# Later weight loads, an earlier load of the last w2 blocks, q units moved ahead and statistics reordered, in a one-core attention and MLP kernel

## The chip, the cores and the metric

The kernel runs on one core of one Trainium2 chip. The metric is device time in microseconds (us) of one execution. Each execution also has a span (first to last instruction, about 1.8 us shorter than the device time) and a mean granted TensorE clock. The highest clock recorded is 1.00, called full clock here; the lowest in any stretch read is 0.50, called half clock.

Engine names in the profile: PE is TensorE (matrix products), PEld its weight loads, DVE is VectorE, ACT is ScalarE, POOL is GpSimd, SP is the engine that issues most DMAs here (SPq in the timeline). L558 means line 558 of the kernel. Names such as `RB`, `OTR` or `yT` are buffers of the kernel; `OTR` receives the transposed attention output. PE writes its products to `ps_all`, a buffer in PSUM that the kernel divides into banks of 512 columns.

## The reference

One sequence of 2048 tokens, width 576, 32 heads of 18, MLP width 4608, bfloat16:

```python
def _A_ref(x, wqkv, w_phi, wo):              # linear attention with learned features
    q, k, v = ...                            # x @ wqkv, split into heads
    pq = einsum("bhsd,hdf->bhsf", q, w_phi)  # the same for k: pk
    phi_q = concatenate([softmax(pq), softmax(-pq)])   # the same for k: phi_k
    kv = einsum("bhsf,bhsd->bhfd", phi_k, v)
    z  = einsum("bhsf->bhf", phi_k)
    o = einsum("bhqf,bhfd->bhqd", phi_q, kv) / (einsum("bhqf,bhf->bhq", phi_q, z) + 1e-6)
    return merge_heads(o) @ wo
def _B_ref(x, w1, b1, w2, b2):               # MLP, with its own layernorm
    return gelu(layernorm(x) @ w1 + b1) @ w2 + b2
h  = x + _A_ref(layernorm(x), A_wqkv, A_w_phi, A_wo)
h2 = h + _B_ref(layernorm(h), B_w1, B_b1, B_w2, B_b2)
```

## The kernel before

The tokens are 16 tiles of 128. There are four stages.

1. Preparation (to 12 us): x and weights arrive, the k weights are multiplied by w_phi ("weffk").
2. The kv loop (12 to 81 us): per tile a layernorm, a transpose of the normed tile (`yT`), the k product (L558), its exponentials on ACT (L565), the v product (L574), and the accumulation of kv (L609). Between them stand the weffq units (L487, L493), and then "q units" (L639): products whose exponentials (L645, on ACT) give Eq for attention.
3. A short chain to W1 (81 to 103 us): attention and output product of tiles 0 and 1, and the remaining q units.
4. Eight rounds of W1 and W2, some 39 us each, with the attention of later tiles woven in.

A helper records every operation, works out its waits from what it reads and writes, and leaves each engine's program in the order of the calls. So order is all that the change edits. In the loop, `t` is the tile and NT is 16. The parts that it touches (cut):

```python
    def ln1_stats_act(t):     # mean and square sum on ACT (L362, L364), four small POOL operations
    def ln1_stats_dve(t):     # the same by bn_stats on DVE, two small POOL operations
    def ln1_norm(eng, t):     # ybuf = (x - mean) * rstd (L390)
    def ln1_tr(t):            # yT(t) = transpose of ybuf by DMA, issued on SP
    def ln1_petr(t, col):     # the same on PE (L425) with a copy on ACT (L429)
    def fill(n, banks):       # the next n q units, their PSUM banks in turn
    ...
    WU = {2: (0, 1), 3: (2, 3), 4: (4, 5, 6)}
    for t in range(NT):
        for u in ((4, 5) if t == 1 else (t + 4,) if 1 < t < NT - 4 else ()):
            ln1_norm("pool", u)
        p1_k(t)               # L558, L565
        if t == 0:
            p1_v(0)
            ln1_petr(1, 512 * 6)
        if t == 1:
            ln1_petr(2, 512 * 6)
        ... weffq units, fill(1) from tile 5, p1_v(t - 1), p1_kv(t - 2) ...
        for u in ((4, 5) if t == 1 else (t + 4,) if 1 < t < NT - 4 else ()):
            ln1_tr(u)
        if t == 1:
            ln1_stats_act(6)
        elif t % 2 == 1 and t + 5 < NT:
            ln1_stats_act(t + 5)
        ... p1_mul(t - 1), p1_sums(t) on DVE ...
        if t == 0:
            ln1_stats_act(4)
            ln1_stats_dve(5)
        elif t % 2 == 0 and t + 5 < NT:
            ln1_stats_dve(t + 5)
        if t == 1:
            ... two DMA transposes of b1, on SP ...
        if t >= 1 and bulk:   # 18 loads: w1, wo, first w2 blocks, b2; on SP
            bulk.pop(0)()
        if t >= 1 and t % 4 == 0 and bulk:
            bulk.pop(0)()
    p1_v(NT - 1, 0); p1_kv(NT - 2); p1_mul(NT - 1, 0)
    fill(2, (4, 3))
    p1_kv(NT - 1)
    ...
    fill(3, QB2)
    attn_oT(0, S1)            # transpose on PE, copy on ACT
    y0 = attn_wo(0, S1, True) # output product L754, then DVE
    attn_oT(1, S2)
    fill(1, QB2)
    y1 = attn_wo(1, S2, True)
    fill(24, QB2)             # all that are left
    attn_yT(y0, ...); attn_yT(y1, ...)
    attn_N(2, S1)             # attention product L659 of tile 2, then DVE, POOL, DMA transpose
    ... load the last 16 w2 blocks (2 x 1152 KB) on SP ...
```

The softmax here doesn't subtract the row's maximum and nothing guards it: scores larger than these inputs give would overflow.

Of the kernel before, what the change touches and what calls it, by code (L numbers as in the profile page):

```python
# [185 lines left out]
def _build(nc, A_x, A_wqkv, A_w_phi, A_wo, B_w1, B_b1, B_w2, B_b2, out):  # L186
# [6 lines left out]
    NT = S // 128  # L193
# [17 lines left out]
    def hap(t, row, off, dims, np_=128):  # L211
        return bass.AP(t, off, [[row, np_]] + [list(d) for d in dims])
# [18 lines left out]
    NW2B = 16  # L231
# [3 lines left out]
    wv = RB[:, 0:2880].rearrange("p (c f) -> p c f", c=5)  # L235
    Ek = [RB[:, 2880 + ES * i:2880 + ES * (i + 1)] for i in range(3)]
    VO = 2880 + 3 * ES
    vext = [RB[:, VO + 1216 * i:VO + 1216 * (i + 1)] for i in range(2)]
    wkst = w2a[:, 0:6, :].rearrange("p m d -> p (m d)")[:, 0:3200].rearrange("p (c k) -> p c k", c=5)
    w2b = RB[:, 0:NW2B * D].rearrange("p (m d) -> p m d", m=NW2B)  # L240
# [36 lines left out]
    def res(name):  # L277
        if name not in R:
            R[name] = Res(name)
        return R[name]  # L280
# [38 lines left out]
    def load(q, dst, src, writes, reads=()):  # L319
        ch = P.chan(f"ld{nch[0]}", q)  # L320
        nch[0] += 1
        P.dma(ch, lambda e: e.dma_start(dst, src), reads=reads, writes=writes)
# [36 lines left out]
    def ln1_stats_act(t):  # L359
        s, w = res(f"s1a{t}"), res(f"s1b{t}")  # L360
        st = lambda k: st1[:, k, t:t + 1]
        P.add("act", lambda e: e.activation(junk[:, 0, :], x_all[:, t, :], AF.Copy, scale=1.0 / D, accum_out=st(6)),  # L362
              reads=[res(f"x{t}")], writes=[s, res("junk0")])
        P.add("act", lambda e: e.activation(junk[:, 1, :], x_all[:, t, :], AF.Square, scale=float(D) ** -0.5,  # L364
                                            accum_out=st(1)),
              reads=[res(f"x{t}")], writes=[s, res("junk1")])
        P.add("pool", lambda e: e.tensor_tensor(st(2), st(6), st(6), ALU.mult), reads=[s], writes=[w])
        P.add("pool", lambda e: e.tensor_tensor(st(7), st(1), st(2), ALU.subtract), reads=[s, w], writes=[w])
        P.add("pool", lambda e: e.tensor_scalar(st(4), st(7), EPS, None, ALU.add), reads=[w], writes=[w])
        P.add("pool", lambda e: e.tensor_tensor(st(5), st(4), neghalf[:, 0:1], ALU.pow),  # L370
              reads=[w, res("neghalf")], writes=[w])

    def ln1_stats_dve(t):
        s, w = res(f"s1a{t}"), res(f"s1b{t}")
        for i in range(2):
            P.add("dve", lambda e, i=i: e.bn_stats(bns[:, 6 * i:6 * i + 6], x_all[:, t, 288 * i:288 * i + 288]),
                  reads=[res(f"x{t}")], writes=[res("bns")])
        P.add("dve", lambda e: e.bn_aggr(hap(st1, 8 * NT, 6 * NT + t, [[NT, 2]]), bns[:, :]),
              reads=[res("bns")], writes=[s])
        P.add("pool", lambda e: e.tensor_scalar(st1[:, 4, t:t + 1], st1[:, 7, t:t + 1], EPS, None, ALU.add),  # L380
              reads=[s], writes=[w])
        P.add("pool", lambda e: e.tensor_tensor(st1[:, 5, t:t + 1], st1[:, 4, t:t + 1], neghalf[:, 0:1], ALU.pow),  # L382
              reads=[w, res("neghalf")], writes=[w])
# [14 lines left out]
    def tr_y(yb, t):  # L398
        sl = t % NSL
        dma_tr(yT[:, :, sl * 128:(sl + 1) * 128], ybuf[yb][:, :], [res(f"ybuf{yb}"), res(f"ybufd{yb}")],  # L400
               [res(f"yT{sl}")])
# [9 lines left out]
    def ln1_norm(eng, t):  # L411
        yb1[t] = norm(eng, x_all[:, t, :], res(f"x{t}"), st1[:, 6, t:t + 1], st1[:, 5, t:t + 1], (res(f"s1b{t}"),))

    def ln1_tr(t):
        tr_y(yb1[t], t)
# [17 lines left out]
    def ln1_petr(t, col, eng="act"):  # L433
        sl, yb = t % NSL, yb1[t]
        pe_tr(ybuf[yb], yT[:, :, sl * 128:(sl + 1) * 128], col, [res(f"ybuf{yb}"), res(f"ybufd{yb}")],
              [res(f"yT{sl}")], eng)
# [85 lines left out]
    bulk = []  # L522
# [15 lines left out]
    NW2A = NF - NW2B  # L538
# [198 lines left out]
    def attn_oT(t, bset=None):  # L737
        ob = t % 2
        rd = [res(f"obuf{ob}"), res(f"opad{ob}")]
        wr = [res(f"oT{ob}")] + (WPH + [res("phib"), res("mask25")] if t < 2 else [])  # L740
        if bset is None:
            dma_tr(oT[ob], obuf[ob][:, :], rd, wr)
        else:
            pe_tr(obuf[ob], oT[ob], 512 * bset[2], rd, wr, dup=True)
# [58 lines left out]
    def fill(n, banks=(4,)):  # L803
        for _ in range(n):
            if qlist:
                r, u = qlist.pop(0)
                q_unit(r, u, banks[qn[0] % len(banks)])
                qn[0] += 1

    WU = {2: (0, 1), 3: (2, 3), 4: (4, 5, 6)}  # L810
    for t in range(NT):
        last = t == NT - 1
        for u in ((4, 5) if t == 1 else (t + 4,) if 1 < t < NT - 4 else ()):
            ln1_norm("pool", u)
        p1_k(t)
        if t == 0:
            p1_v(0)
            ln1_petr(1, 512 * 6)
        if t == 1:
            ln1_petr(2, 512 * 6)  # L820
        for i in WU.get(t, ())[:1]:
            weffq_unit(i)
        if t >= 5:
            fill(1)
        if t >= 2:
            p1_v(t - 1)
        for i in WU.get(t, ())[1:2]:
            weffq_unit(i)
        if t >= 2:
            p1_kv(t - 2)  # L830
        for i in WU.get(t, ())[2:]:
            weffq_unit(i)
        for u in ((4, 5) if t == 1 else (t + 4,) if 1 < t < NT - 4 else ()):
            ln1_tr(u)
        if t == 1:
            ln1_stats_act(6)
        elif t % 2 == 1 and t + 5 < NT:
            ln1_stats_act(t + 5)
        if t >= 1:
            p1_mul(t - 1)  # L840
        p1_sums(t)
        if t == 0:
            ln1_stats_act(4)
            ln1_stats_dve(5)
        elif t % 2 == 0 and t + 5 < NT:
            ln1_stats_dve(t + 5)
        if t == 1:
            dma_tr(b1st[:, 0:32].rearrange("p (o k) -> p o k", o=1),
                   B_b1[0:4096].rearrange("(m p) -> m p", p=128), [], [res("b1a")])
            dma_tr(b1st[:, 32:48].rearrange("p (o k) -> p o k", o=1),  # L850
                   B_b1[2560:4608].rearrange("(m p) -> m p", p=128), [], [res("b1b")])
        if t == 13:
            P.add("pool", lambda e: e.tensor_copy(b1T[:, 0:32], b1st[:, 0:32]), reads=[res("b1a")], writes=[res("b1T")])
            P.add("pool", lambda e: e.tensor_copy(b1T[:, 32:36], b1st[:, 44:48]), reads=[res("b1b")], writes=[res("b1T")])
        if t >= 1 and bulk:
            bulk.pop(0)()
        if t >= 1 and t % 4 == 0 and bulk:
            bulk.pop(0)()
    p1_v(NT - 1, 0)
    p1_kv(NT - 2)  # L860
    p1_mul(NT - 1, 0)
    fill(2, (4, 3))
    p1_kv(NT - 1)
    while bulk:
        bulk.pop(0)()
# [6 lines left out]
        kvr[:, :, 25:32, 0:19], ps_kv(512 * 7, [[133, 2], [19, 7], [1, 19]]),  # L872
        mask7[:, :, :].unsqueeze(1).to_broadcast([128, 2, 7, 19]), ALU.mult),
        reads=[res("mask7")], writes=[res("kvrb")], banks=[bank[7]])

    S1, S2 = (6, 7, 5), (1, 2, 0)
    QB2 = (4, 3)
# [10 lines left out]
    attn_N_mul(1, S2, 1, "dve")  # L888
    fill(3, QB2)
    attn_oT(0, S1)  # L890
    y0 = attn_wo(0, S1, True)
    attn_oT(1, S2)
    fill(1, QB2)
# [4 lines left out]
    attn_N(2, S1)  # L898
    P.add("act", lambda e: e.activation(sums[0][:, 0:1], neghalf[:, 0:1], AF.Gelu_apprx_tanh),
          reads=[res("neghalf")], writes=[res("sums0")])  # L900

    RB_OLD = ([res(f"Ekpad{i}") for i in range(3)] + [res(f"vext{i}") for i in range(2)] +
              [res(f"vext{i}b") for i in range(2)] + [res(f"Ek{i}_{s}") for i in range(3) for s in range(2)] +
              [res("wv"), res("wv4"), res("wvpad")])
    for m0 in range(0, NW2B, 8):
        load("sp", w2b[:, m0:m0 + 8, :],
             B_w2[128 * (NW2A + m0):128 * (NW2A + m0 + 8), :].rearrange("(m p) d -> p m d", p=128),
             [res(f"w2_{NW2A + m}") for m in range(m0, m0 + 8)] + (RB_OLD if m0 == 0 else []))


    RA_OLD = rr("wkT{}", 5) + rr("wqT{}", 5) + [res("wkTpad"), res("wqTpad")] + R_weffk
# [107 lines left out]
    for r in range(NR):  # L1019
        a, b = RT * (r + 1), RT * (r + 1) + 1  # L1020
        extra, slots = {}, ({}, {})
        if r + 1 < NR:
            ia, ib = (3, 12) if r else (9, 15)
            for t, i in ((a, ia), (b, ib)):
                extra[i] = [(*wo_half(t, S1, 0), None)]
                extra[i + 1] = [(*wo_half(t, S1, 1), lambda t=t: attn_wo(t, S1))]
            if r == 0:
                extra[3] = [((), (), lambda: attn_N(b, S1))]
        if r + 2 < NR:
            slots[0][2] = lambda: attn_N(a + RT, S1)  # L1030
            slots[1][6] = lambda: attn_N(b + RT, S1)
        w1_round(r, extra)
        w2_tile(r, 0, slots[0])
        w2_tile(r, 1, slots[1])
# [34 lines left out]
```

## Time and profile before

| | |
|---|---|
| device time | 422.36 us, median of 3 (420.44 to 423.21); the profiled execution 418.99 us |
| span, clock | 417.1 us, 0.999 |
| PE busy | 95% of the span |
| from 125 us on | PE idle about 0.3 us per 39 us round |

From the page of the kernel before: busy time per engine, and the busy tenths of PE and DMA in 40 slices of about 10.4 us.

```profile
PE 396.5 (95%) x4957; PEld 289.9 (70%) x4998; DVE 180.5 (43%) x449; ACT 181.8 (44%) x420; POOL 104.1 (25%) x144
...
PE   7688999977999999999999999999999999999996
...
DMA  9359994500381111111011101101111130100000
```

PE is the limit. Its larger holes are in the first slices (the early tiles) and in slices 9 and 10 (the chain to W1). Outside the holes a faster engine elsewhere should gain nothing (PE has 84% of the chain that ended last); a filled hole should be worth its length, as far as no later wait takes it back.

The timeline of the kernel before names the holes. Columns: start, duration, engine, line, operation; in brackets the idle time before it and what ended it.

```profile
36.80 1.39 PE L558 MATMUL ps_all<-RA,yT 128*128 128x512 bf16 x10 [1.11 <-ACT tpn L364]
...
80.53 0.73 PE L609 MATMUL ps_all<-RB 128*128 128x133 bf16 x10 [0.79 <-DVE RB L595]
...
88.48 0.57 PE L425 MATMUL ps_all<-ident,obuf 128*128 128x128 bf16 x6 [1.32 <-DVE obuf L723]
...
90.01 1.54 PE L754 MATMUL ps_all<-wo_sb,OTR 64*128 64x288 bf16 x18 [0.96 <-ACT OTR L429]
...
102.67 0.74 PE L659 MATMUL ps_all<-kvr,Eq 126*128 126x140 bf16 x10 [1.06 <-ACT yT L429]
...
122.11 0.29 PE L754 MATMUL ps_all<-wo_sb,OTR 64*128 64x288 bf16 x1 [1.01 <-DMA OTR<-obuf]
```

The first is the k product of tile 6. The profile blames an ACT statistic, but the code has no such wait. What the product needs is the DMA transpose of tile 6. SP's timeline shows when that was issued:

```profile
29.60 0.58 SPq L322 DMA_DIRECT2D w1sb<-in_B_w_dram  x1
30.27 1.22 SPq L336 DMA_TRANSPOSE yT<-ybuf  x1
```

The DMA view of 29.5 to 30.9 us gives its landing (last number: us from issue to landing):

```profile
yT<-ybuf SPq DMA_TRANSPOSE x1, 6.4
```

The transpose was issued behind a 576 KB load and landed after 6.4 us, at 36.7 us; the one issued at 18.99 us, before any of the bulk loads, landed in 2.6 us, which is also the median of all 27 transposes of `yT` in that trace.

On ACT the exponentials of tiles 2 and 3 (L565) stood as follows, with the second weffq copy between them:

```profile
20.60 1.19 ACT L565 ACTIVATE RB<-ps_all 128x576 bf16<-128x576 f32 x2
...
22.76 0.55 ACT L493 ACTIVATE WQ<-ps_all 128x450 bf16<-128x450 f32 x1 [0.53 <-PE ps_all L487]
24.55 1.19 ACT L565 ACTIVATE RB<-ps_all 128x576 bf16<-128x576 f32 x2 [1.24 <-PE ps_all L558]
```

ACT had 1.24 us to spare before tile 3.

### The profile page before, as it was taken

The numbers are of one execution on the slowest core, as the hardware profiler recorded it, in microseconds if no ns is written. First come the engines' busy times: TensorE is split into PE (matmuls) and PEld (weight loads), VectorE is DVE, ScalarE is ACT, GpSimd is POOL, SyncE is SP. The second block draws the span as 40 slices with busy tenths as digits, with TensorE's granted clock in tenths as the row PEclk, the third lists the DMA queues.
The fourth block names the chain that finished last, engine by engine and source line by source line (L and its number), as shares of the span: only waits on it lengthen the run. The fifth ranks groups of instructions, "written<-read, shape, count | busy, mean of one in ns | idle before, by whom it ended". The sixth has DMA issues, their size and how long they took to land.

```text
span 417.1 us, 11635 instructions
## 1 busy us (share of the span) xinstructions
PE 396.5 (95%) x4957; PEld 289.9 (70%) x4998; DVE 180.5 (43%) x449; ACT 181.8 (44%) x420; POOL 104.1 (25%) x144
## 2 busy tenths in 40 slices
PE   7688999977999999999999999999999999999996
PEld 3455666755875598569757965995598569758953
DVE  5886997794525423432540254223423432300000
ACT  3976765457772066017402730462066017404710
POOL 4798881011303200220022022002200220111001
PEclk9999999999999999999999999999999999999999
DMA  9359994500381111111011101101111130100000
GB/s 254 73 156 275 232 200 127 195 2 2 79 201 27 37 29 21 31 32 19 17 31 31 19 17 30 31 20 34 30 28 22 31 31 19 17 14 18 2 2 28
DMA packets 44923, 25.71 MB, mean 62 GB/s; under 512 B 32072, under 2 KB 43848, under 8 KB 44872
## 3 DMA queue, kind: packets, MB, share of 16 engines
q1 hardware_dynamic: 44112, 24.80, 24.8%
q8 instruction: 39, 0.64, 0.6%
q10 hardware_dynamic: 760, 0.17, 0.3%
q14 instruction: 12, 0.10, 0.1%
HBM read 15.13 MB, written 2.36 MB: 42 GB/s over the span
## 4 chain that ended last, share of the span: by engine, by line
PE 84%; ACT 8%; DMA 3%; DVE 2%; issue 2%; ACTq 0%; SPq 0%; DVEq 0%
PE ps_all L1004 33%; PE ps_all L936 30%; PE ps_all L754 5%; PE ps_all L558 4%; PE ps_all L639 4%; PE ps_all L574 3%; ACT RA L947 2%; PE ps_all L659 2%; DMA OTR<-obuf 2%; PE ps_all L609 2%; ACT RB L565 1%; DMA w2a<-in_A_wqkv_dram 1%; ACT Eq L645 1%; ACT tpn L364 1%; ACT tpn L362 1%
## 5 line engine op out<-in xcount | busy, mean ns | idle before, releaser
L947 ACT ACTIVATE RA<-ps_all,b1T 128x256 bf16<-128x256 f32 x288 | 115.0, 479 | 178.5 <-PE ps_all L936 162.1
L936 PE MATMUL ps_all<-yT,w1sb 64*128 64x256 bf16 x2304 | 152.4, 269 | 0.0
L936 PEld LDWEIGHTS ps_all<-yT,w1sb 64*128 64x128 bf16 x2304 | 136.2, 94 | 5.1
L1004 PE MATMUL ps_all<-w2a,RA 128*128 128x512 bf16 (+1 forms) x624 | 93.9, 284 | 2.0 <-ACT RA L947 1.1
L936 PE MATMUL ps_all<-yT,w1t 64*128 64x256 bf16 x288 | 70.9, 270 | 0.0
L1004 PEld LDWEIGHTS ps_all<-w2a,RA 128*128 128x128 bf16 x640 | 45.9, 98 | 35.6 <-ACT RA L947 1.7
L1004 PE MATMUL ps_all<-RB,RA 128*128 128x512 bf16 (+1 forms) x498 | 66.6, 284 | 0.4
L1013 DVE TENSOR_TENSOR WQ<-ps_all,tmpo 128x64 bf16<-128x64 f32 (+1 forms) x32 | 14.7, 458 | 101.4 <-PE ps_all L1004 92.2
L1004 PEld LDWEIGHTS ps_all<-RB,RA 128*128 128x128 bf16 x512 | 33.5, 98 | 32.2
L773 DVE SCALAR_TENSOR_TENSOR x_all<-ps_all,x_all 128x576 bf16<-128x576 f32 x16 | 12.1, 758 | 82.4 <-PE ps_all L754 82.4
L785 POOL TENSOR_TENSOR st<-st,neghalf 128x1 f32<-128x1 f32 x16 | 8.8, 551 | 135.5 <-DVE st L787 135.5
L723 POOL TENSOR_TENSOR obuf<-tpn 128x576 bf16<-128x576 f32 x14 | 19.6, 1401 | 90.3 <-DVE tpn L718 79.8
L754 PE MATMUL ps_all<-wo_sb,OTR 64*128 64x288 bf16 x288 | 29.7, 283 | 2.2 <-DMA OTR<-obuf 1.0
L1010 POOL TENSOR_TENSOR tmpo<-x_all,b2bc 128x576 f32<-128x576 bf16 x16 | 20.4, 1273 | 43.6 <-DVE WQ L1013 43.6
L390 POOL TENSOR_SCALAR ybuf<-x_all,st 128x576 bf16<-128x576 bf16 x13 | 29.9, 2303 | 2.3 <-POOL st L382 1.2
L645 ACT ACTIVATE Eq<-ps_all 128x512 bf16<-128x512 f32 (+1 forms) x48 | 25.3, 527 | 8.6 <-PE ps_all L639 7.7
L936 PEld LDWEIGHTS ps_all<-yT,w1t 64*128 64x128 bf16 x288 | 26.3, 94 | 1.9
L565 ACT ACTIVATE RB<-ps_all 128x576 bf16<-128x576 f32 x32 | 19.1, 647 | 16.6 <-PE ps_all L558 16.6
L639 PE MATMUL ps_all<-yT,WQ 128*128 128x256 bf16 x200 | 25.0, 273 | 1.3 <-ACT Eq L645 1.3
L558 PE MATMUL ps_all<-RA,yT 128*128 128x64 bf16 (+1 forms) x155 | 21.1, 283 | 4.5 <-ACT yT L429 2.4
L595 DVE TENSOR_TENSOR RB<-ps_all,RB 128x1152 bf16<-128x1152 f32 x16 | 21.5, 1343 | 8.0 <-PE ps_all L574 7.9
L754 PEld LDWEIGHTS ps_all<-wo_sb,OTR 64*128 64x128 bf16 x288 | 19.5, 94 | 5.4 <-DMA OTR<-obuf 1.3
(104 smaller groups left out, 322.1 us busy)
## 6 DMA issues: line engine op xcount, KB each, us to landing
w1sb<-in_B_w_dram SPq DMA_DIRECT2D x8, 576.0 KB, 5.2
w2a<-in_B_w_dram SPq DMA_DIRECT2D x4, 720.0 KB, 5.9
RB<-in_B_w_dram SPq DMA_DIRECT2D x2, 1152.0 KB, 7.9
out_dram<-WQ SPq DMA_DIRECT2D x16, 144.0 KB, 1.7
x_all<-in_A_x_dram SPq DMA_DIRECT2D x3, 576.0 KB, 4.9
w2a<-in_A_wqkv_dram SPq DMA_DIRECT2D x2, 288.0 KB, 4.0
RB<-in_A_wqkv_dram SPq DMA_DIRECT2D x1, 576.0 KB, 5.4
w1t<-in_B_w_dram SPq DMA_DIRECT2D x2, 288.0 KB, 4.7
```

Of the source, the lines that this page charges most:

```text
L390: P.add(eng, lambda e: e.tensor_scalar(ybuf[yb][:, 0:D], src, mean, rstd, ALU.subtract, ALU.mult), reads=[r_src, *r_st], writes=[res(f"ybu ...
L558: P.add("pe", lambda e, c=c, o=o, n=n: e.matmul(ps_all[:, 512 * KB + o:512 * KB + o + n], yT[:, c, sl * 128:(sl + 1) * 128], weffk[:, c, o ...
L565: P.add("act", lambda e, s=s: e.activation(Ek[eb][:, D * s:D * s + D], ps_all[:, 512 * KB:512 * KB + D], AF.Exp, scale=1.0 if s == 0 else ...
L595: P.add("dve", lambda e: e.tensor_tensor(vx(t)[:, :, :, 0:DH], ps_all[:, 512 * VB:512 * VB + D].rearrange("p (h d) -> p h d", h=H).unsquee ...
L639: P.add("pe", lambda e, i=i, c=c, h0=h0: e.matmul(ps_all[:, 512 * bk + RW * i:512 * bk + RW * i + RW], weffq[:, c, DH * h0:DH * h0 + 128], ...
L645: P.add("act", lambda e, s=s: e.activation(Eq[:, r, s, bs[0]:bs[0] + n, :], ps_all[:, 512 * bk:512 * bk + RW * n].rearrange("p (b t) -> p ...
L723: P.add(oeng, lambda e: e.tensor_tensor(obuf[ob][:, 0:D], tpn[:, 0, :], tpn[:, 1, :], ALU.add), reads=[res("tpn")], writes=[res(f"obuf{ob}")])
L754: P.add(lane, lambda e: e.matmul(ps_all[:, 512 * bk:512 * bk + DHF], oT[ob][h:h + 64, c, :], wo_sb[h:h + 64, c, o:o + DHF], start=first, s ...
L936: P.add(lane, lambda e: e.matmul(ps_all[:, o:o + RW], lhs, yT[h:h + 64, c, ys], start=first, stop=not begin and i == 1 and c == 3, skip_gr ...
L947: P.add("act", lambda e, m=m, o=o: e.activation(hmid[:, m, :], ps_all[:, o:o + RW], AF.Gelu_apprx_tanh, bias=b1T[:, m:m + 1]), reads=[res( ...
L1004: P.add("pe", lambda e, m=m, bk=bk, o=o, n=n: e.matmul(ps_all[:, 512 * bk:512 * bk + n], w2_lhs(m, j), w2_rhs(m, o, n), start=(m == 0), st ...
L1010: P.add("pool", lambda e: e.tensor_tensor(tmpo[:, :], x_all[:, t, :], b2bc[:, :], ALU.add), reads=[res("b2"), res(f"x{t}")], writes=[res(" ...
```

## The change

Its intent: no bulk load in front of the early transposes; statistics out of ACT's way in the first tiles; q units into PE's holes, so that fewer stand in the chain to W1; the last w2 blocks loaded while DMA is idle (0 in slices 9 and 10 above), not in round 0. The diff is shortened:

```diff
-        for u in ((4, 5) if t == 1 else (t + 4,) if 1 < t < NT - 4 else ()):
-            ln1_norm("pool", u)
+        if 1 < t < NT - 4:
+            ln1_norm("pool", t + 4)
+        if t == 1:
+            ln1_petr(2, 512 * 6)
         p1_k(t)
 ...
         if t == 1:
-            ln1_petr(2, 512 * 6)
+            ln1_stats_act(4)
+            ln1_norm("pool", 4)
+            ln1_tr(4)
 ...
-        if t == 1:
-            ln1_stats_act(6)
-        elif t % 2 == 1 and t + 5 < NT:
-            ln1_stats_act(t + 5)
+        if t == 2:
+            ln1_stats_act(8)
+        elif t > 2 and t % 2 == 1 and t + 7 < NT:
+            ln1_stats_act(t + 7)
 ...
-        if t == 0:
-            ln1_stats_act(4)
+        if t == 1:
             ln1_stats_dve(5)
+            ln1_norm("pool", 5)
+            ln1_tr(5)
+            ln1_stats_dve(6)
 ...
-        if t == 1:
+        if t == 5:
             (the two transposes of b1)
-        if t >= 1 and bulk:
+        if t >= 4 and bulk:
             bulk.pop(0)()
-        if t >= 1 and t % 4 == 0 and bulk:
+        if t >= 5 and t % 2 == 1 and bulk:
             bulk.pop(0)()
 ...
-    fill(2, (4, 3))
+    fill(3, (4, 3))
     p1_kv(NT - 1)
 ...
+    (load of the last w2 blocks, moved here from behind attn_N(2, S1))
 ...
     attn_oT(0, S1)
+    fill(1, QB2)
     y0 = attn_wo(0, S1, True)
 ...
-            ia, ib = (3, 12) if r else (9, 15)
+            ia, ib = (3, 12) if r else (9, 16)
```

The last line moves the output product of tile 3 from slot 15 to slot 16 of the 18 slots of round 0.

More of the change, by code (lines that the diff above doesn't have):

```diff
@@ L832, in _build @@
             weffq_unit(i)
-        for u in ((4, 5) if t == 1 else (t + 4,) if 1 < t < NT - 4 else ()):
-            ln1_tr(u)
-        if t == 1:
-            ln1_stats_act(6)
-        elif t % 2 == 1 and t + 5 < NT:
-            ln1_stats_act(t + 5)
+        if 1 < t < NT - 4:
+            ln1_tr(t + 4)
+        if t == 2:
+            ln1_stats_act(8)
+        elif t > 2 and t % 2 == 1 and t + 7 < NT:
+            ln1_stats_act(t + 7)
         if t >= 1:
@@ L841, in _build @@
         p1_sums(t)
-        if t == 0:
-            ln1_stats_act(4)
+        if t == 1:
             ln1_stats_dve(5)
-        elif t % 2 == 0 and t + 5 < NT:
+            ln1_norm("pool", 5)
+            ln1_tr(5)
+            ln1_stats_dve(6)
+        elif t % 2 == 0 and t >= 2 and t + 5 < NT:
             ln1_stats_dve(t + 5)
-        if t == 1:
+        if t == 5:
             dma_tr(b1st[:, 0:32].rearrange("p (o k) -> p o k", o=1),
@@ L874, in _build @@
         reads=[res("mask7")], writes=[res("kvrb")], banks=[bank[7]])
+    RB_OLD = ([res(f"Ekpad{i}") for i in range(3)] + [res(f"vext{i}") for i in range(2)] +
+              [res(f"vext{i}b") for i in range(2)] + [res(f"Ek{i}_{s}") for i in range(3) for s in range(2)] +
+              [res("wv"), res("wv4"), res("wvpad")])
+    for m0 in range(0, NW2B, 8):
+        load("sp", w2b[:, m0:m0 + 8, :],
+             B_w2[128 * (NW2A + m0):128 * (NW2A + m0 + 8), :].rearrange("(m p) d -> p m d", p=128),
+             [res(f"w2_{NW2A + m}") for m in range(m0, m0 + 8)] + (RB_OLD if m0 == 0 else []))
     S1, S2 = (6, 7, 5), (1, 2, 0)
@@ L900, in _build @@
           reads=[res("neghalf")], writes=[res("sums0")])
-    RB_OLD = ([res(f"Ekpad{i}") for i in range(3)] + [res(f"vext{i}") for i in range(2)] +
-              [res(f"vext{i}b") for i in range(2)] + [res(f"Ek{i}_{s}") for i in range(3) for s in range(2)] +
-              [res("wv"), res("wv4"), res("wvpad")])
-    for m0 in range(0, NW2B, 8):
-        load("sp", w2b[:, m0:m0 + 8, :],
-             B_w2[128 * (NW2A + m0):128 * (NW2A + m0 + 8), :].rearrange("(m p) d -> p m d", p=128),
-             [res(f"w2_{NW2A + m}") for m in range(m0, m0 + 8)] + (RB_OLD if m0 == 0 else []))
     RA_OLD = rr("wkT{}", 5) + rr("wqT{}", 5) + [res("wkTpad"), res("wqTpad")] + R_weffk
```

## The prediction

> What bounds the kernel now. TensorE (PE) is busy 396.5 of 417.1 us, with 84% of the chain of waits, clock 0.999. From 125 us on it idles about 0.3 us per 39 us round (stretches view), so the change, which touches only the first 125 us, can win only from PE's gaps there. The timeline shows them: 0.8 and 1.6 us before the k products of tiles 1 and 2 (ACT copy of yT), 1.1 before tile 6 (36.8 us), 0.8 before the last kv (80.5 us), some 5.5 between 86 and 103 us, 1.0 at 122 us (DMA OTR<-obuf).
>
> 1. Later bulk loads. The transpose of tile 6 is issued at 30.27 us behind a 576 KB w1 load (29.60) and lands after 6.4 us; unloaded ones take 2.6. [...] Without loads before tile 8 the 1.1 us gap goes. The loads still finish near 73 us, before W1.
>
> 2. Statistics reordered. The transposes of tile 2 move into the 0.8 us gap before tile 1, and statistics of tile 4 no longer precede tile 1's exponentials: tile 2 starts 0.6 us sooner. But ACT statistics of tile 8 (1.57 us) now stand before tile 3's exponentials, and x of tile 8 lands only at about 24.3 us (issued 20.26, 4.0 us). ACT should reach it near 22.8 us, wait, and finish at 25.9; those exponentials started at 24.55 before. Stages 3 and 4 are paced by ACT (weff copies), so tiles 4 and 5 come about 1.5 us later. Parts 1 and 2 together: tile 6 near 37.4 us instead of 36.8, a loss of 0.6 us.
>
> 3. q units ahead. One more unit (1.1 us PE) fills the gap before the last kv but delays the attention vector chain by about 0.7 us; one fills the 1.0 us wait for the ACT copy of OTR. Three units remain instead of five after the second wo product, where ACT's Eq exponentials (1.23 us per unit) hold PE. Recounted with traced durations, the attention product of tile 2 starts near 100.5 us instead of 102.67: gain 2.2 us.
>
> 4. w2 blocks at the last kv. They (2 x 1152 KB, 7.9 us) now land near 89 us, on an idle DMA. The transpose of obuf at 113.97 us, behind them before (8.1 us), lands in about 2.6: the gap at 122 us goes. But the wo product moves to the last unit of round 0, and the attention product two W2 products later needs its banks back from the VectorE add (0.76 us): I expect a new gap of 0.6 us. Net gain 0.5 us.
>
> Sum: +0.6 - 2.2 - 0.5 = -2.1 us, 0.5%. Predicted 420.3 us, range 417.0 to 422.8; runs before spread over 2.8 us. Faster by over 2%: 0.01; within 2%: 0.98; slower by over 2%: 0.01.
>
> What would show it: no PE wait on a landing at tile 6; an ACT wait on x_all of about 1.5 us near 23 us; the first W1 product near 101 us plus the loss of part 2 (before 103.33); no OTR wait at 121 us but a short PE idle before the L659 product after the first W2 products; rounds 1 to 7 unchanged at 39.1 us.
>
> What would make it wrong: x of tile 8 landing earlier (1.5 us better); POOL, almost full from 15 to 45 us (2.3 us per norm), falling behind so that tiles 7 to 9 wait; the q units' banks holding PE longer before attention than I count.

Part 1 rests on the two landings, 6.4 and 2.6 us.

## The result, and the profile after

| | before | after |
|---|---|---|
| device time, median | 422.03 us (4 executions, 420.44 to 423.21) | 417.48 us (4 executions, 416.57 to 417.89) |
| ratio of means | | 0.9892, 95% interval 0.9854 to 0.9929 |
| span and clock of the profiled execution | 417.1 us, 0.999 | 415.7 us, 0.995 |

A ratio is the mean time of one kernel's fast runs over that of the other's of the same rounds, so it isn't quite the ratio of the medians.

The time lies inside the predicted range, but there is a puzzle: the medians differ by 4.5 us, the two traced spans only by 1.4 us. The profiled execution of before (418.99 us) is faster than the four timed beside it.

The page of the kernel after:

```profile
PE 400.7 (96%) x4998; PEld 290.2 (70%) x4998; DVE 181.7 (44%) x452; ACT 180.6 (43%) x416; POOL 103.8 (25%) x142
...
PE   7779999988999999999999999999999999999996
...
DMA  8352697690111100111011001101110120100000
```

PE's 400.7 us are not comparable with 396.5: the trace of before has 4957 of 4998 products, and a part of the products of after ran at half clock.

ACT in the kernel after, at the same place:

```profile
22.13 0.55 ACT L493 ACTIVATE WQ<-ps_all 128x450 bf16<-128x450 f32 x1 [0.53 <-PE ps_all L487]
24.78 0.68 ACT L362 ACTIVATE tpn<-x_all 128x576 f32<-128x576 bf16 x1 [2.10 <-DMA x_all<-in_A_x_dram]
...
26.27 1.17 ACT L565 ACTIVATE RB<-ps_all 128x576 bf16<-128x576 f32 x2
```

This is the predicted stall. The statistics of tile 8 now stand before the exponentials of tile 3, and wait 2.10 us for x of tile 8. Those exponentials start at 26.27 us instead of 24.55. On PE it becomes a hole of 2.5 us:

```profile
27.93 0.38 PE L487 MATMUL ps_all<-OTR,RA 126*128 126x126 bf16 x4 [2.51 <-ACT WQ L493]
28.15 0.72 PE L609 MATMUL ps_all<-RB 128*128 128x133 bf16 x10
28.71 2.07 PE L558 MATMUL ps_all<-RA,yT 128*128 128x512 bf16 x10
```

The k product behind it takes 2.07 us, where ten such products took 1.39 us in the line at 36.80 us of before. The view of busy time by stretches shows why: the last but two numbers of a line are the granted clock (then DMA share and GB/s).

```profile
28.00:30.00 2.00, 2.00 (x21) 1.26 (x22) 1.91 (x3) 1.56 (x4) 1.82 (x2) 0.81 0.42 82
30.00:32.00 2.00, 2.00 (x13) 1.13 (x12) 0.00 (x0) 1.55 (x5) 1.75 (x5) 0.50 0.02 5
32.00:34.00 2.00, 1.97 (x22) 1.21 (x20) 0.71 (x1) 1.06 (x3) 1.74 (x4) 0.83 0.43 85
```

The clock fell to half behind the hole, for about 3.4 us. In stretches of 0.2 us the same trace shows a clock of 1.00 up to 29.2 us, 0.50 from 29.4 to 32.6 us, and 1.00 again from 32.8 us. If it is either 1.00 or 0.50, a mean of 0.81 over 2 us is 0.76 us at half, 0.50 is 2 us, 0.83 is 0.68 us; where I give the length of a half clock below, it is estimated in this way.

The k product of tile 6, the chain to W1 and the first round, after:

```profile
38.26 1.39 PE L558 MATMUL ps_all<-RA,yT 128*128 128x512 bf16 x10
...
83.77 1.27 PE L639 MATMUL ps_all<-yT,WQ 128*128 128x256 bf16 x10 [0.33 <-ACT Eq L645]
...
90.61 0.57 PE L425 MATMUL ps_all<-ident,obuf 128*128 128x128 bf16 x6 [0.71 <-DVE obuf L723]
...
101.97 0.74 PE L659 MATMUL ps_all<-kvr,Eq 126*128 126x140 bf16 x10 [0.94 <-ACT yT L429]
...
121.22 0.28 PE L754 MATMUL ps_all<-wo_sb,OTR 64*128 64x288 bf16 x1
...
124.73 0.48 PE L659 MATMUL ps_all<-kvr,Eq 126*128 126x140 bf16 x5 [0.33 <-DVE x_all L773]
```

The wait at tile 6 is gone. The holes before the last kv product and before the first output product are gone or smaller. The wait on OTR at 122 us is gone. In its place is the predicted wait of the attention product on the VectorE add (0.33 us). So where did the other 3 us of the medians come from?

### The profile page after: what moved, and what is told of

Its sections match the earlier page's. It is cut to its first block, busy times and chain, and to the rows that moved or that the text cites. A ratio compares the mean times of both kernels' runs of the same rounds, so it can differ in the third digit from the quotient of the medians.

```text
span 415.7 us, 11671 instructions
## 1 busy us (share of the span) xinstructions
PE 400.7 (96%) x4998; PEld 290.2 (70%) x4998; DVE 181.7 (44%) x452; ACT 180.6 (43%) x416; POOL 103.8 (25%) x142
## 4 chain that ended last, share of the span: by engine, by line
PE 89%; DVE 3%; DMA 2%; ACT 2%; POOL 1%; issue 1%; SPq 1%; DVEq 0%; ACTq 0%; POOLq 0%
PE ps_all L943 34%; PE ps_all L1011 34%; PE ps_all L754 5%; PE ps_all L574 4%; PE ps_all L558 4%; PE ps_all L639 3%; PE ps_all L659 2%; PE ps_all L609 2%; DMA x_all<-in_A_x_dram 1%; DMA w2a<-in_A_wqkv_dram 1%; ACT Eq L645 1%; DVE x_all L773 1%; POOL ybuf L390 1%; PE ps_all L445 0%; PE ps_all L487 0%
## 5 line engine op out<-in xcount | busy, mean ns | idle before, releaser
L1011 PE MATMUL ps_all<-w2a,RA 128*128 128x512 bf16 (+1 forms) x640 | 96.2, 286 | 0.0
L1011 PE MATMUL ps_all<-RB,RA 128*128 128x64 bf16 (+1 forms) x512 | 67.7, 286 | 0.0
L754 PE MATMUL ps_all<-wo_sb,OTR 64*128 64x288 bf16 x288 | 29.7, 283 | 0.4 <-ACT OTR L429 0.2
L943 PEld LDWEIGHTS ps_all<-yT,w1t 64*128 64x128 bf16 x288 | 26.3, 94 | 1.9
L558 PE MATMUL ps_all<-RA,yT 128*128 128x512 bf16 (+1 forms) x160 | 22.9, 291 | 1.9 <-ACT RB L565 1.3
L574 PE MATMUL ps_all<-RB,yT 128*128 128x512 bf16 (+1 forms) x160 | 23.1, 293 | 0.0
```

Source lines behind the costliest of these rows:

```text
L558: P.add("pe", lambda e, c=c, o=o, n=n: e.matmul(ps_all[:, 512 * KB + o:512 * KB + o + n], yT[:, c, sl * 128:(sl + 1) * 128], weffk[:, c, o ...
L574: P.add("pe", lambda e, c=c, o=o, n=n: e.matmul(ps_all[:, 512 * VB + o:512 * VB + o + n], yT[:, c, sl * 128:(sl + 1) * 128], wv[:, c, o:o ...
L754: P.add(lane, lambda e: e.matmul(ps_all[:, 512 * bk:512 * bk + DHF], oT[ob][h:h + 64, c, :], wo_sb[h:h + 64, c, o:o + DHF], start=first, s ...
L943: P.add(lane, lambda e: e.matmul(ps_all[:, o:o + RW], lhs, yT[h:h + 64, c, ys], start=first, stop=not begin and i == 1 and c == 3, skip_gr ...
L1011: P.add("pe", lambda e, m=m, bk=bk, o=o, n=n: e.matmul(ps_all[:, 512 * bk:512 * bk + n], w2_lhs(m, j), w2_rhs(m, o, n), start=(m == 0), st ...
```

## The experiments

Two theories for the gap between 1.4 and 4.5 us, as they stood after e1 (the recorded text of e1 uses the letters A and B for earlier ones). Theory A: the schedule itself gains only 1 to 2 us; the rest is that the executions of before were disturbed more often, by half clock of TensorE or late landings. Theory B: the schedule gains 4 us and the trace of before was untypical. Beside these, each part of the change is priced alone, and the two costs that it brought are undone.

All executions but the four of before beside the result list their clock. One stretch of 3.4 us at half clock lowers the mean over 417 us by 0.004, so I read 0.996 or 0.995 as one stretch and 0.992 as two. The traces agree, as far as their clock was read (to 130 us): those with 0.995 or 0.996 (after, e1, e3, e4, g1) have one stretch, h2 with 0.992 has two, at 9 to 13 us and at 91 to 95 us, and those with 0.999 or 1.0 have none. Of executions without a trace it is an estimate. I call an execution undisturbed when its clock is 0.998 or more and it is within 2 us of that kernel's fastest; why the second condition is needed is shown under f2. This filter was chosen after seeing the data, so the table gives both kinds of mean. "Before" pools the 50 executions with a clock on record (44 timed beside the runs, 6 of e1; not the four beside the result), "after" pools 10 (4 of the result, 6 of f1).

| kernel | all: mean us | clock 0.998 or more | undisturbed: mean us (number) |
|---|---|---|---|
| before | 420.6 | 11 of 50 | 418.6 (10) |
| after | 417.4 | 7 of 10 | 417.1 (7) |
| e2: before + w2 blocks early | 418.2 | 3 of 6 | 417.5 (3) |
| e3: before + q units ahead | 417.2 | 4 of 6 | 416.7 (4) |
| e4: before + statistics and loads | 421.2 | 1 of 6 | 420.1 (1) |
| h2: before + late loads alone | 419.2 | 1 of 6 | 417.6 (1) |
| f4: before + dummy products | 419.1 | 5 of 6 | 418.4 (4) |
| f2: after, statistics of tile 8 later | 416.6 | 5 of 6 | 416.0 (4) |
| f3: f2 + slot 15 | 416.5 | 5 of 6 | 415.2 (4) |
| g1: f3 + dummy products in another bank | 415.6 | 5 of 6 | 415.2 (5) |
| g2: f3 + early loads | 414.7 | 6 of 6 | 414.7 (6) |
| h1: g2 and g1 together | 414.6 | 5 of 6 | 414.0 (5) |

All twelve runs gave correct results.

### e1_before_again: the kernel before against itself

No edit.

> The kernel before, unchanged, against itself. The two profiled spans differ by only 1.4 us (417.1 before, 415.7 after) while the medians differ by 4.5 us (422.0, 417.5), and the profiled run of the kernel before (419.0 us) is faster than every timed one (420.4 to 423.2). Theory A: the kernel before has a stall that varies from run to run, probably where DMA transposes queue behind bulk loads; then its runs spread over 2 us or more again, and the new trace has a PE gap of 1 us or more that the first trace lacks. Theory B: the first trace is typical and the difference is outside the span or chance; then the new trace has the same gaps within 0.3 us and the mean lies near 419 us. Ratio 1.00 either way.

Measured: ratio 0.9981 (0.9929 to 1.0033). The executions spread from 419.4 to 421.6 us, those of before in the same rounds from 418.4 to 424.1. Two of the six had full clock, two 0.995 or 0.996, two 0.991 or 0.992. The new trace (418.5 us span, clock 0.996) shows one disturbance that the first lacks, in the chain to W1:

```profile
86.00:88.00 2.00, 0.72 (x5) 0.41 (x5) 1.93 (x4) 1.91 (x4) 0.00 (x0) 1.00 0.00 0
88.00:90.00 2.00, 1.00 (x14) 0.69 (x16) 1.86 (x5) 0.74 (x2) 0.00 (x0) 1.00 0.00 0
90.00:92.00 2.00, 1.91 (x18) 0.82 (x14) 1.30 (x3) 0.00 (x0) 0.00 (x0) 0.64 0.00 0
92.00:94.00 2.00, 2.00 (x12) 1.37 (x12) 1.71 (x7) 0.70 (x1) 0.16 (x1) 0.51 0.00 0
```

PE was busy 1.72 of 4 us (first number in each line after the length), in the two waits at L425 and L754, and then its clock was half for some 3.4 us (0.64 and 0.51 in the last two lines). The output product took 1.97 us instead of 1.54. From the end of the first wait to the attention product of tile 2 it took 15.6 us (88.04 to 103.66) instead of 14.2 us (88.48 to 102.67). So one such stretch costs about 1.4 us here. The expected new wait of 1 us or more on a landing did not appear: OTR cost 1.44 us against 1.01, and tile 6 cost 0.10 us against 1.11 (with 0.36 us at tile 4). The largest difference between the two traces was the clock, which neither theory had named for this run.

The wait at tile 6 isn't constant either: it was 0.99 us in e2, 0.31 in e3 and 0.86 in f4, all with the loads of before.

### e2_w2_early, e3_q_ahead, e4_prep_only: the parts alone

e2 moves the load of the last w2 blocks behind the last kv product; slot 15 stays. e3:

```diff
-    fill(2, (4, 3))
+    fill(3, (4, 3))
 ...
     attn_oT(0, S1)
+    fill(1, QB2)
```

e4 takes all edits of the kv loop (statistics, loads, b1) and nothing else.

> Kernel before with only the last w2 blocks loaded at the last kv. My sum: the 1.0 us PE gap at 122 us goes, nothing replaces it (the wo product stays at slot 15): 1.0 us faster, ratio 0.9976, and no PE wait on OTR. Rival (most of the measured 4.5 us comes from here, because the landing behind 2.3 MB varies from run to run): 2 us or more faster, ratio 0.995 or less, and a smaller spread of times.

> Kernel before with only the two q units moved ahead. Prediction: about 2.2 us faster (ratio 0.995), the attention product of tile 2 near 100.5 us. Rival: the after trace still shows 0.83 and 0.71 us gaps before attention, where the moved unit waits for its bank, and ACT works through the same exponentials; only about 1 us is gained (ratio 0.9976).

> Kernel before with only the reordered statistics and the later bulk loads; q units, w2 blocks and slot 15 as before. Prediction: 0.6 us slower (ratio 1.0014); the after trace, with a 2.5 us PE gap at 25 us, says up to 1.5 us slower (1.0035). Rival: if the unsteady part of the kernel before lies in its bulk loads at tiles 4 to 8, this is 1 us or more faster (ratio 0.9976 or less) and its times spread less.

Measured, ratios to before: e2 0.9924 (0.9877 to 0.9971), e3 0.9901 (0.9855 to 0.9947), e4 0.9996 (0.995 to 1.0042). Those of e2 and e3 alone would add up to more than the whole change; before was disturbed more often than either. By its ratio e2 met the mark of its rival (0.995 or less), but the traces with the load in round 0 don't bear the rival out: the wait on OTR was 1.44 us in e1 and e4, 1.00 in e3, 1.01 in f4 and 0.97 in h2, so it varied by 0.5 us, not by 2. Undisturbed, the parts are worth -1.1 us (e2), -1.9 us (e3) and +1.5 us (e4, from one execution only). Their sum, -1.5 us, is what after gains over before undisturbed (417.1 against 418.6 us); that the two agree so closely is in part chance, since e4 is one execution and slot 16 is in none of the three. The traces agree roughly. From the first k product to the attention product of tile 2, before took 90.3 us and e3 87.5 us; of these 2.8 us, 0.8 us are a shorter wait at tile 6 in that execution (0.31 us against 1.11), 2.0 us the q units. In the undisturbed trace of after (f1) the same stretch took 89.4 us: the new kv loop gave 1.9 us back against e3. In e4's own trace it took 91.6 us, 1.3 us more than before. In e2 PE has no wait on OTR at all. The span from the attention product of tile 2 to the end fell from 314.4 us to 313.2 us.

The traces of e3 and e4 (clock 0.996 and 0.995) also have a half clock, but at another place. In e3 it shows at the three dummy products that stand before the weff products, and in the stretches there:

```profile
9.49 1.46 PE L312 MATMUL ps_all<-WQ 128*128 128x512 bf16 x3 [0.80 <-ACT yT L429]
```

```profile
8.00:10.00 2.00, 1.20 (x12) 0.62 (x9) 1.87 (x5) 1.22 (x2) 0.00 (x0) 0.87 1.10 366
10.00:12.00 2.00, 2.00 (x16) 1.45 (x15) 0.55 (x5) 0.55 (x1) 1.70 (x6) 0.50 1.39 94
12.00:14.00 2.00, 1.46 (x18) 1.22 (x16) 1.56 (x3) 1.37 (x4) 0.84 (x3) 0.78 1.03 204
```

It begins behind a hole of 0.80 us, a place that the change does not touch. So a half clock of before need not lie in the chain to W1.

### f1_after_again: the kernel after, once more

No edit.

> The kernel after, unchanged, on the chip of this call. Executions of the kernel before with clock 0.999 or more took 418.4 to 418.6 us, of the kernel after 416.6 and 417.6. Theory: the schedule alone gains 1.5 to 2 us, as predicted; the rest of the measured 4.5 us is that the kernel before had more windows of half TensorE clock (0.004 of clock each, 1 to 2 us) and late landings in the executions compared. Then the executions with clock 0.999 or more differ by 1.5 to 2 us here too, and the ratio of all is between 0.989 and 0.995. Rival: a schedule gain of 4 us that the one trace of before hid; then the undisturbed executions differ by 3 us or more.

Measured: ratio 0.993 (0.9891 to 0.9968), median 417.18 us. Five of the six executions had full clock and lie between 417.09 and 417.36 us. The three of before with full clock took 418.68, 418.21 and 422.88 us, the last with a disturbance that the clock does not show. Without that one the difference is 1.3 us, a little less than the 1.5 to 2 us expected. The rival (theory B) fell: undisturbed, the kernels differ by 1.5 us (pooled), not 3 or more. Of the pooled difference of all executions, 3.2 us, some 1.7 us are disturbances.

### f4_before_busy: PE kept busy in the two waits

The helper's definition is cut:

```diff
     fill(3, QB2)
+    keep_busy(3)      # 512-column products of constant data into PSUM bank 7, never read
     attn_oT(0, S1)
+    keep_busy(4)
     y0 = attn_wo(0, S1, True)
```

> Kernel before with seven 512-column dummy products (0.22 us each) put into the two waits between 86 and 90 us, where PE only waits for VectorE and ACT; results unchanged. Theory: idle PE there lets the clock fall to half in some executions, for about 3.4 us (the second trace of before shows 0.5 at 92 us); with PE kept busy this stops: executions with full clock stay at 418.5 us, but the share of them grows, the mean falls by about 0.5 to 1 us (ratio 0.998). Rival: the dips come at any time, whatever the gaps: same mean, same number of dips as before.

Measured: ratio 0.997 (0.9931 to 1.0009), so the means alone decide nothing. But five of six executions had full clock, against 3 of 11 of before in the same rounds and 11 of 50 in all, and the undisturbed time stayed at 418.4 us. The dummy products stand in the waits of the timeline (the 0.22 us each of the expectation is their distance in the trace of before, where three start at 9.46 us and the next product at 10.11; here three took 0.81 us and four 1.04):

```profile
90.18 0.81 PE L893 MATMUL ps_all<-w1sb,ident 128*128 128x512 bf16 x3 [0.61 <-DVE tpn L718]
...
91.39 1.04 PE L893 MATMUL ps_all<-w1sb,ident 128*128 128x512 bf16 x4
```

Its stretches at the same place as those of e1:

```profile
92.00:94.00 2.00, 1.89 (x21) 0.74 (x20) 1.85 (x3) 0.36 (x1) 0.00 (x0) 1.00 0.00 0
94.00:96.00 2.00, 2.00 (x22) 1.48 (x24) 1.75 (x5) 0.92 (x2) 0.00 (x0) 1.00 0.00 0
```

The clock stays at 1.00 where e1 had 0.51 (f4's trace runs some 2.5 us later, so these windows cover the same products). One trace shows little, but the counts and the traces together speak for it: with PE kept busy there, fewer executions had a half clock. The q units that the change moves ahead fill the same place. The eight kernels with them, counting the result and f1 as two, had full clock in 37 of 46 executions; before and the kernels without q units moved ahead or dummies in 16 of 68. Of the five traces without either, two have a half clock in the chain to W1 (e1, h2); of the nine with, none has. So in these runs half clock came less often where PE's idle time there was filled (with f4 42 of 52 executions at full clock, against 16 of 68); by what mechanism isn't shown. Where the half clock lay in the executions without a trace isn't on record.

### f2_stats8_later, f3_stats8_slot15: undoing the two new waits

f2 is the kernel after with

```diff
-        if t == 2:
-            ln1_stats_act(8)
-        elif t > 2 and t % 2 == 1 and t + 7 < NT:
-            ln1_stats_act(t + 7)
+        if t > 2 and t % 2 == 1 and t + 5 < NT:
+            ln1_stats_act(t + 5)
```

f3 is f2 with `(9, 15)` instead of `(9, 16)`.

> Kernel after with the ACT statistics of tile 8 back at tile 3 (and 10, 12, 14 at 5, 7, 9), so that ACT no longer waits 2.1 us for x of tile 8. Theory: the 2.5 us PE gap at 25 us shrinks to about 0.4 us and with it the half clock behind it goes: 1.5 to 2.5 us faster than f1, about 415 us, ratio to before 0.986. Rival: the wait is absorbed elsewhere (POOL or the copies of weff hold tiles 3 to 5 anyway): no difference from f1.

> As f2, with the wo product of round 0 back at slot 15. The PE gap of 0.33 us before the attention product at the start of the first W2 goes: 0.3 us faster than f2, within the noise; the trace shows no PE wait on the VectorE add there. If the landing of OTR were late, a PE wait on OTR would come instead, up to 1 us.

Measured: f2 0.9911 (0.9874 to 0.9948), undisturbed 416.0 us, 1.1 us better than after; f3 0.9907 (0.9861 to 0.9953), undisturbed 415.2 us. In both traces the wait at L487, 2.5 us in the result and 2.0 in f1, is down to under 0.2 us. New waits on transposes took up a part: 0.52 us (f2) and 0.44 us (f3) at tile 4, 0.35 and 0.98 us at tile 10. So f2 gained less than the 1.5 to 2.5 us expected. In f3 the wait of L659 on the VectorE add is gone (0.33 us), and none on OTR came. f3's other 0.5 us over f2 is not explained by this edit.

The trace of f2 (418.31 us, clock 1.0) shows one way in which an execution can be slow at a recorded full clock. Its first products, with L445 the transposes of the k weights:

```profile
5.84 3.52 PE L445 MATMUL ps_all<-ident,w2a 128*128 128x128 bf16 x23 [0.30 <-DMA w2a<-in_A_wqkv_dram]
...
10.81 1.46 PE L312 MATMUL ps_all<-WQ 128*128 128x512 bf16 x3 [0.80 <-ACT yT L429]
```

and those of f3, whose program is the same up to here:

```profile
5.70 2.49 PE L445 MATMUL ps_all<-ident,w2a 128*128 128x128 bf16 x23 [0.15 <-DMA w2a<-in_A_wqkv_dram]
...
9.37 0.82 PE L312 MATMUL ps_all<-WQ 128*128 128x512 bf16 x3 [0.80 <-ACT yT L429]
```

In f2 PE ran slower here: three 512-column products took 1.46 us instead of 0.82, and the first k product came at 15.05 us instead of 12.11. The clock records show nothing of it (1.00 in every stretch), yet 1.46 us is what the same three products took in e3, e4 and h2, whose records have the half clock there (0.50 at 10 to 12 us). So f2 most likely ran its start at half clock, unrecorded; this is my estimate from the durations. The trace of f4 has the same start (1.46 us for the three, the first k product at 14.85 us). Such a start costs 2.7 to 2.9 us and can probably happen to every kernel here: all run the same program up to these dummies, and only g1 and h1 change even their bank. That the executions of before at 422 to 424 us contain one is likely, but they left no trace, so it is not shown.

### h2_loads_late_only and g2_loads_early: are later loads a gain?

h2 is before with the two `bulk` conditions of the change; b1 stays at tile 1. g2 is f3 with the two `bulk` conditions of before; b1 stays at tile 5.

> As f3, with the bulk loads issued as in the kernel before (one per tile from tile 1, a second at tiles 4, 8, 12). Theory: the wait of 0.7 to 1.0 us at tile 11 (loads three per two tiles before it) goes, and a wait of up to 1.1 us at tile 5 or 6 comes back (transpose behind the first w1 loads): undisturbed executions within 0.5 us of f3. Rival: later loads are worth the full 1.1 us: 1 us slower than f3.

> Kernel before with only the bulk loads begun three tiles later (the two b1 transposes stay at tile 1). The part of the prediction on trial: the wait of about 1 us at tile 6 goes for nothing else, 1.1 us faster when undisturbed (417.4 us). After g2 against f3 I expect otherwise: the wait at tile 6 goes and one of 0.7 to 2 us before tile 11 comes, undisturbed executions at 418.2 to 419 us, no gain.

Measured: g2 0.9851 (0.982 to 0.9883), undisturbed 414.7 us, all six at full clock. That is 0.5 us better than f3 with late loads (f3 ran on another chip; g1, which is f3 but for a bank, ran beside g2 and is 0.5 us behind it too). The wait at tile 6 came back, as expected: 0.54 us in g2's trace, 0.72 in h1's. h2 0.9974 (0.994 to 1.0008), its one undisturbed execution 417.6 us, 1.0 us better than before. Here my expectation for h2 was wrong and the prediction's part 1 right, as far as one undisturbed execution and one trace show: alone, later loads remove the wait at tile 6 and bring none later. Together with the reordering they bring one: 0.69 us in f1, 0.82 in e4, 0.98 in f3, 2.06 in g1. The expectations call it tile 11; counting the k products shows that it is tile 10. SP's timeline of f1 shows how it arises:

```profile
44.34 3.12 SPq L336 DMA_TRANSPOSE b1st<-in_B_b_dram  x2
47.51 1.05 SPq L322 DMA_DIRECT2D w1sb<-in_B_w_dram  x2
48.66 1.32 SPq L336 DMA_TRANSPOSE yT<-ybuf  x1
```

and PE's, with the k product of tile 10:

```profile
54.05 1.39 PE L558 MATMUL ps_all<-RA,yT 128*128 128x512 bf16 x10 [0.69 <-DMA yT<-ybuf]
```

SP's timeline of h2:

```profile
42.91 1.04 SPq L322 DMA_DIRECT2D w1sb<-in_B_w_dram  x2
45.54 1.20 SPq L336 DMA_TRANSPOSE yT<-ybuf  x1
```

The two b1 transposes, moved to tile 5, hold SP for 3.1 us. The two loads behind them go out at 47.51 us, and right behind these the transpose of tile 10 at 48.66 us, though its normed tile was ready at 46.7 us. It lands after 5.3 us, at 54.0 us, and the product starts. In h2 the same transpose goes out at 45.54 us and lands after 4.6 us, well before its product (52.44 us). That the position of b1 is the cause is read from the traces; b1 alone was not tried. In g2 b1 stands at tile 5 too, but only one load goes before the transpose of tile 10 (issued 47.07 us, landed after 4.3 us), and its product doesn't wait.

A half clock also followed this wait, once: behind the 2.06 us of g1 the ten products of the k product took 2.46 us, with a granted clock of 0.50 at 54 to 56 us.

### g1_warm_bank0 and h1_best

g1 is f3 with the three dummy products that stand before the weff products written to PSUM bank 0, which is free by then, and not to bank 6, which ACT still reads (the helper's new parameter is cut):

```diff
-    warm(3)
+    warm(3, 0)
```

h1 is g2 with the same edit.

> As f3, with the three dummy products after the first transposes written to PSUM bank 0, which is free, instead of bank 6, which ACT still reads. Theory: PE's 0.8 us idle before them (8.7 to 9.4 us) goes and the weff products start up to 0.8 us earlier; undisturbed executions at about 414.5 us (f3: 415.1 to 415.4), and starts with half clock between 9 and 14 us (seen in two traces) become rarer[...]. Rival: the weff products wait for the copies of wkT or the mask anyway, or POOL holds the tiles: same time as f3.

> g2 and g1 together: loads early, statistics of tile 8 late, slot 15, dummy products in bank 0. Theory: about 0.3 us faster than g2, undisturbed executions near 414.2 us, no half clock between 9 and 14 us; ratio to before 0.984. Rival: POOL and the landing of x set the early tiles, no change from g2 (414.6 us).

Measured: g1 0.9872 (0.9839 to 0.9905), undisturbed 415.2 us, no change from f3, with the wait of 2.06 us at tile 10 in its trace. h1 0.9869 (0.9833 to 0.9906), undisturbed 414.0 us, 0.7 us better than g2 (on another chip). In both traces the 0.8 us before the dummies is gone, but the first k product then waits 1.1 us instead of 0.6. Only about 0.3 us is gained at the start; the rest of h1's 0.7 us is not accounted for, and may lie between the two calls. One h1 execution (417.36 us, clock 0.995) was disturbed all the same. h1 beats both kernels; its median of 414.19 us compares with 419.5 us of before in its rounds. g2 (414.60 us) and h1 can't be told apart by their ratios.

## Why the prediction was right or wrong

The range held, and the class (within 2%) too: 417.48 us against 420.3 predicted, 417.0 to 422.8. The centre was 2.8 us too high. That the range held is in part luck. The prediction started from 422.4 us, the median of three executions, while the mean of 50 was 420.6 us: 1.8 us of the error. Fewer disturbances after the change made 1.7 us more, which no step of the prediction had. The schedule gained 0.6 us less than predicted, which took a part of the error back. One of the four executions after (416.57 us) lies below the range. Point by point:

1. "Without loads before tile 8 the 1.1 us gap goes": right. h2, which does only this, has no such wait and gains 1.0 us in its one undisturbed execution. Missed: with the two b1 transposes moved to tile 5 and two loads behind them, tile 10 waits instead, by 0.7 us in f1. With the reordering, later loads were a small loss where it was tried (g2 against f3: 0.5 us).

2. "ACT should reach it near 22.8 us, wait, and finish at 25.9": right. ACT got there at 22.7 us, waited 2.10 us for x of tile 8, and finished at 26.3. The net of parts 1 and 2 was mis-sized: +0.6 us predicted, +1.5 us measured (e4, one execution; 1.9 us by the traces of f1 and e3). Up to tile 6 the sum held: its k product starts at 37.36 us in f1, predicted near 37.4 (at 38.26 us in the result, where the half clock lies before it). x landed at 24.8 us instead of 24.3. What the sum lacked is the wait at tile 10: 0.69 us in f1, 0.82 in e4, none in the result.

3. q units, "gain 2.2 us": 1.9 us measured (e3). The mechanism held, with a new wait of 0.33 us and fewer exponentials at the end; the wait of 0.83 us on an exponential (88.63 us) isn't new but moved, for before had it at 97.40 us.

4. w2 blocks: -1.0 for the gap and +0.6 for the new wait predicted; -1.1 (e2) measured for the first, 0.33 us of wait for the second in the trace.

The sum for the schedule was thus -2.1 us predicted and -1.5 us measured. What was missing is a term of its own. The prediction treated PE's clock as constant ("clock 0.999") because the one trace of before showed it so. In most executions of before it was not: 39 of 50 had, by their mean clock, one or more stretches at half clock, and with PE's idle time in the chain to W1 filled most of them were gone. All disturbances together are worth about 1.7 us in the mean of all executions. The recorded half clock makes an estimated 0.8 to 1.3 us of it: by the clocks, before had about 1.1 stretches per execution and after 0.3, and a stretch cost 1.0 us in the result (27.93 us to the k product of tile 5, against f1), 1.4 in e1 and 1.7 in g1 (from the k product of tile 10 to the next, against f1). The rest is open; slow starts as in f2 would fit. The 4.5 us between the first two medians also contain chance: later medians of before were 419.5 to 421.6 us, and the clocks of the four executions of before were not recorded.

In the traces a half clock lasts about 3.4 us each time (after, e1, e3, e4, g1, twice in h2; the lowest clock of a 2 us stretch is 0.50 or 0.51), stands behind holes, and appears in some executions and not in others. What sets off the fall in one execution and not in another isn't shown (see the last section).

The landings that part 1 rested on came again: behind the same 576 KB load the transpose took 5.8 us in e1 and 6.3 in e2, against 6.4 in before and 2.6 without such a load.

## What to carry to other kernels

Look at the spread and the clock of all executions before believing one trace. Here holes of PE cost their length and, in some executions, a half clock behind them: another 1.0 us behind a hole of 2.5 us (after), 1.4 us behind 2.3 us in two holes (e1), 1.7 us behind 2.06 us (g1). So useful work put into a hole can gain more than the hole: e3 gained 1.9 us undisturbed and 3.4 us in the mean of all executions. Dummy products gained at most the half clock: f4's undisturbed time stayed as it was (418.4 us against 418.6). When work is moved ahead in an engine's program, ask when its data land, as with tile 8 here (ACT waited 2.10 us), and what the moved item holds up behind it, as with b1 (SP was held for 3.1 us).

## What the traces show of the clock and of SP

- Idle time before a half clock: one hole of 2.5 us (after) or 2.06 us (g1), 2.3 us in two holes within 2.9 us (e1 and the second stretch of h2), and in e3, e4 and the first stretch of h2 a hole of 0.80 us. No half clock followed a hole of 2.02 us (f1), the same two holes of 1.32 and 0.96 us in before and e2, or the 0.80 us in the other executions traced at full clock, so the length of the hole alone does not decide it.
- The clock records may miss a half clock. The runs give a likely instance: f2 and f4 record a mean clock of 1.0, while their first products ran at some 1.8 times the usual duration (1.46 us instead of 0.82 for three, as in e3 at a recorded half clock) and the first k product came 2.7 to 2.9 us late.
- In these traces a DMA transpose held SP for longer than a load did: one of a 128x640 tile held it for 1.2 us or more and the two of b1 for 2.5 to 3.4 us, against mostly about 0.6 us for a 576 KB load.
